# Loading one piece of wo over 121 partitions instead of 128, with other cuts of wo and twelve unread products on PE

## The chip, the core and the metric

The kernel runs on one core of a Trainium2 chip. A core has five engines that run their own instruction lists: PE (TensorE, matrix products), DVE (VectorE), ACT (ScalarE), POOL (GpSimd) and SP (SyncE, which here only issues transfers). Transfers between the chip's memory and the core's SBUF are done by 16 DMA engines. The metric is the device time of one execution in microseconds (us); a smaller number is better.

## The reference

For four sequences and one new token each, the result is a gated mix of two branches of the same input x (4 x 1 x 512):

```
g = sigmoid(sum(x * gate_w))                        # one number for each sequence
a: q = x @ wq                                       # 32 heads of 128
   k, v = the last 4096 rows of the caches          # 8 heads, each shared by 4 heads of q
   a = softmax(q k^T / sqrt(128)) v  @ wo           # wo is 4096 x 512
b: gate = x @ W_gate; up = x @ W_up                 # 512 x 1792
   b = (gate * (gate > 0) * up) @ W_down            # 1792 x 512
out = g * a + (1 - g) * b
```

All inputs and the output are bfloat16. Some 81 MB are read once (the used part of the caches is 64 MB of it), and little is computed with each byte.

## The kernel before, in words

The kernel's instruction lists are written out by hand. A small class, Program, collects the operations of each engine in order (`op` and `dma`) with the names of the events that each waits for; `emit` turns the names into waits on semaphores. What stands first in an engine's list runs first.

**Transfers.** SP issues nearly all loads on one queue, in this order: wq; the keys K of set 0 and 1 and so on in turn with the values V, eight sets (a set is one sequence and half of its heads, 4 MB of keys and 4 MB of values); W_gate and W_up; the last values; W_down (`Wd`); and last wo in pieces (line 286). A piece covers all 128 partitions and some of the 32 rows of 512 elements that each partition holds: `WO_CUTS = (0, 18, 26, 30, 32)` makes pieces of 18, 8, 4 and 2 rows. wo lands in the memory of `KT`, which holds the turned keys before; so SP waits until the scores of the last set are done (`("SC", NSET - 1, 1)`) before it issues wo's pieces. Each piece has an event of its own, `("WO", k)`. ACT issues the two small loads of x and gate_w at the start (lines 272 and 273).

**Each of eight sets.** DVE turns the keys (line 376), PE makes the scores (L384), DVE and PE find the maximum, ACT takes the exponential into `p` (L402), PE spreads `p` with the constant `perm` into four banks of PSUM (L405), ACT copies and DVE turns them, and PE multiplies them with V into `OB` (L426). DVE adds up `OB` (L435, L438). PE runs the eight sets as a loop, with what follows behind it.

**The end, on PE, in order.** After the last set: 14 products of branch b with `Wd` into the bank `SB` (`grouped`, L517); `select` (L442), which gathers the attention's result; DVE's `normal` (L448 to L451: reciprocal, scaling, transpose into `oT`); a transpose on PE (L524); DVE's copy into `oq` (L525). Then come the 18 rows of wo's first piece, as `grouped` products of 512 columns, four column groups of the array side by side, added into the same bank `SB` (L517). ACT copies `SB` into `part` (L529). The rest of wo is used in quarters: for each row four products of 128 columns into four corners of the bank `AB` (L536), row by row as the pieces land. After the second piece's rows, four products with the constant `S32` (L542, 32-bit, two instructions each) add `part` to `AB`. After the last row DVE and ACT copy the four corners to `outr` (L547), and SP stores it (L567).

```
for k in range(1, len(WO_CUTS) - 1):              # L533
    for i in range(WO_CUTS[k], WO_CUTS[k + 1]):
        for q in range(4):                        # a product waits for ("WO", k) and ("OQ",)
```

Of the kernel before, what the change touches and what calls it, by code (L numbers as in the profile page):

```python
# [15 lines left out]
NSET = 8  # L16
NFT = FF // 128
# [2 lines left out]
FAR = 1.0e9  # L20
LOWEST = -3.0e38

WO_CUTS = (0, 18, 26, 30, 32)
GROUPED = 18


# [147 lines left out]
def bass_gated_mix__sliding_block_cached__glu_gated_reglu__decode_kernel(  # L174
# [13 lines left out]
    with ExitStack() as ctx:  # L188
        def sb(name, shape, dt):
            return ctx.enter_context(nc.sbuf_tensor(name, shape, dt))  # L190

        def ps(name, width):
            return ctx.enter_context(nc.psum_tensor(name, [128, width], FP32))
# [14 lines left out]
        perm = sb("perm", [128, 4, 128], BF16)  # L208
# [15 lines left out]
        p = sb("p", [128, 512], BF16)  # L224
# [4 lines left out]
        rows = sb("rows", [128, 4], FP32)  # L229
# [3 lines left out]
        oq = sb("oq", [128, 32 * 32], BF16)  # L233
# [4 lines left out]
        OB = ps("OB", 512)  # L238
# [11 lines left out]
        part = Kw[:, 0, 3 * FQ:3 * FQ + 512]  # L250
        Wo = KT[:, :].bitcast(BF16).rearrange("p (i w) -> p i w", w=512)
# [3 lines left out]
        P = Program()  # L255
# [19 lines left out]
        for s in range(1, NSET):  # L275
# [5 lines left out]
        P.dma("sp", lambda e: e.dma_start(Wd[:, :, :].rearrange("p i w -> p (i w)"),  # L281
                                          B_W_down.rearrange("(p i) w -> p (i w)", p=128)), ("WD",))
        wo_src = A_wo.rearrange("(p i) w -> p i w", p=128)
        for k in range(len(WO_CUTS) - 1):
            lo, hi = WO_CUTS[k], WO_CUTS[k + 1]
            P.dma("sp", lambda e, lo=lo, hi=hi: e.dma_start(  # L286
                Wo[:, lo:hi, :].rearrange("p i w -> p (i w)"),
                wo_src[:, lo:hi, :].rearrange("p i w -> p (i w)")), ("WO", k), [("SC", NSET - 1, 1)])

        P.op("pool", lambda e: e.memset(xz[:, :, :].rearrange("p t w -> p (t w)"), 0.0), ("XZ0",))  # L290
        P.op("pool", lambda e: e.memset(onesf[:, :], 1.0), ("ONESF",))
# [47 lines left out]
        for t in range(4):  # L339
            for half in range(2):  # L340
                for g in range(4):
# [3 lines left out]
                        start=(t == 0), stop=(t == 3), tile_position=(0, 32 * g)),  # L345
                        ("Q",) if (half == 1 and t == 3 and g == 3) else None, [("V", -1), ("XT",)])
        P.op("act", lambda e: e.copy(qrow[:, :], PB[:, 0:1024]), ("QR",), [("Q",)], sem="pro")
        for half in range(2):
            for g in range(4):
                P.op("pe", lambda e, half=half, g=g: e.matmul(  # L350
                    PB[:, 512 * g:512 * g + 512], rall[:, 128 * g:128 * g + 128], qrow[:, 512 * half:512 * half + 512],
                    start=True, stop=True), ("R", half) if g == 3 else None,
# [88 lines left out]
        def select(s):  # L441
            P.op("pe", lambda e: e.matmul(FO[0:16, 256:385], S16[:, :], osum[:, :], start=True, stop=True), ("SEL", s),  # L442
                 [("OSB", s), ("S16",)])

        def normal(s):
            b, half = s // 2, s % 2
            r = slice(32 * b, 32 * b + 32)
            P.op("dve", lambda e: e.reciprocal(rc[:, :], FO[0:16, 384:385]), ("RC", s), [("SEL", s)])  # L448
            P.op("dve", lambda e: e.tensor_scalar(on[32 * b:32 * b + 16, :], FO[0:16, 256:384], rc[:, 0:1], gsb[0:16, b:b + 1],
                                                  op0=ALU.mult, op1=ALU.mult), ("ON", s), [("RC", s), ("G",), ("ON0",)])  # L450
            P.op("dve", lambda e: e.transpose(  # L451
                oT[r, 64 * half:64 * half + 128].rearrange("p (j f) -> p f j", f=4),
                on[r, :].rearrange("p (f i) -> p f i", f=4)), ("OT", s), [("ON", s)], sem="vd" if s == NSET - 1 else None)
# [61 lines left out]
        def grouped(n, stat, mov, waits):  # L515
            g = n % 4
            P.op("pe", lambda e: e.matmul(SB[32 * g:32 * g + 32, :], stat, mov, start=(n < 4), stop=(n >= total - 4),  # L517
                                          tile_position=(0, 32 * g)), ("GR",) if n == total - 1 else None, waits)

        for i in range(NFT):  # L520
            grouped(i, hT[:, i:i + 31 * NFT + 1:NFT], Wd[:, i, :], [("WD",), ("H",)])
        select(NSET - 1)
        normal(NSET - 1)
        P.op("pe", lambda e: e.transpose(FO[:, 128:256], oT[:, 0:128], identw[:, :]), ("CB",), [("OT", NSET - 1), ("IDENTW",)])  # L524
        P.op("dve", lambda e: e.tensor_copy(oq[:, 0:128], FO[:, 128:256]), ("OQ",), [("CB",), ("OQ0",)], sem="vd")  # L525
        for i in range(GROUPED):
            k = max(k for k in range(len(WO_CUTS)) if WO_CUTS[k] <= i)
            grouped(NFT + i, oq[:, i:i + 31 * 32 + 1:32], Wo[:, i, :], [("WO", k), ("OQ",)])
        P.op("act", lambda e: e.copy(part[:, :], SB[:, :]), ("PART",), [("GR",)], sem="va")  # L529
        def quarter(q):  # L530
            return AB[32 * q:32 * q + 4, 128 * q:128 * q + 128]

        for k in range(1, len(WO_CUTS) - 1):  # L533
            for i in range(WO_CUTS[k], WO_CUTS[k + 1]):
                for q in range(4):
                    P.op("pe", lambda e, i=i, q=q: e.matmul(  # L536
                        quarter(q), oq[:, i:i + 97:32], Wo[:, i, 128 * q:128 * q + 128],
                        start=(i == GROUPED), stop=(i == 31), tile_position=(0, 32 * q)),
                        ("ACC",) if (i == 31 and q == 3) else None, [("WO", k), ("OQ",)])
            if k == 1:  # L540
                for q in range(4):
                    P.op("pe", lambda e, q=q: e.matmul(quarter(q), S32[:, 0:4], part[:, 128 * q:128 * q + 128],  # L542
                                                       start=False, stop=False, tile_position=(0, 32 * q)), None,
                         [("PART",), ("S32",)])
# [68 lines left out]
```

## Time and profile before

| | us |
|---|---|
| median of three runs (196.69, 196.76, 335.23) | 196.76 |
| the profiled execution | 196.43 |
| its span, from the first to the last instruction | 195.2 |

| engine | busy us | share of the span |
|---|---|---|
| PE | 93.0 | 48% |
| PEld (weight loads, beside PE) | 44.5 | 23% |
| DVE | 116.6 | 60% |
| ACT | 31.6 | 16% |
| POOL | 15.2 | 8% |

The 16 DMA engines moved 81.04 MB at a mean of 415 GB/s. In the page's 40 slices of the span their mean busy share is nine tenths or more in all slices but the first and the last.

How to read the answers: times count from the start of the span, in us. "L517" is line 517 of the kernel before. A row of a timeline has the start, the duration, the engine, the line, the operation, output<-input, shapes and the count; the brackets behind it give the engine's idle time just before and what ended it. PEclk is the share of its full clock that TensorE was granted. The chain of waits follows the work that ended last back to what released it.

### The profile page before, as it was taken

Reading aid. Unit: us, or ns where it says so; the run is one execution under the profiler, and the core shown is the slowest. Engines: PE = TensorE matmul, PEld = TensorE weight load, DVE = VectorE, ACT = ScalarE, POOL = GpSimd, SP = SyncE. Lnnn points to the kernel's source line nnn. Section 1 sums busy time; section 2 is a strip of 40 time slices with the busy share of each in tenths; the row PEclk is TensorE's granted clock in tenths of the full one; section 3 lists DMA queues with packets and bytes.
Section 4 is the critical chain, followed back from the end, with each engine's and each line's share of the span. In section 5 each row is a group of like instructions: output and inputs, shape, how many; then the busy total and the mean of one; then the engine's idle time right before and its main releaser. Section 6 shows DMA issues by size and latency. Waiting matters only on the chain.

```text
span 195.2 us, 2407 instructions
## 1 busy us (share of the span) xinstructions
PE 93.0 (48%) x1005; PEld 44.5 (23%) x1005; DVE 116.6 (60%) x122; ACT 31.6 (16%) x51; POOL 15.2 (8%) x54
## 2 busy tenths in 40 slices
PE   0017525619611961196219611961196229684543
PEld 0012101216101610152016101610151016124212
DVE  0010299699399439943994399449944994264301
ACT  2002360140140014001400140014001400150002
POOL 7007010100100010001000100010001000000000
PEclk9999999666995596579556955596588557955978
DMA  6999999999999999999999999999999999999990
GB/s 215 427 437 450 430 436 450 430 430 436 443 436 430 430 430 436 443 430 430 430 430 430 437 430 430 430 430 430 430 430 430 430 393 432 464 430 403 421 396 24
DMA packets 3494, 81.04 MB, mean 415 GB/s; under 512 B 416, under 2 KB 420, under 8 KB 676
## 3 DMA queue, kind: packets, MB, share of 16 engines
q1 hardware_dynamic: 3464, 81.01, 97.0%
q8 instruction: 1, 0.02, 0.0%
q10 hardware_dynamic: 28, 0.01, 0.0%
q14 instruction: 1, 0.01, 0.0%
HBM read 81.01 MB, written 0.00 MB: 415 GB/s over the span
## 4 chain that ended last, share of the span: by engine, by line
DMA 79%; PE 17%; issue 1%; SPq 1%; ACTq 1%; DVE 0%; DVEq 0%
DMA Vsb<-in_A_v_cache_dram 61%; PE OB L426 13%; DMA KT<-in_A_wo_dram 12%; DMA xs<-in_gate_w_dram 6%; PE SB L384 2%; PE PB L343 2%; SPq L286 1%; ACTq L272 1%; PE FO L330 0%; DVEq L562 0%; DVE xz L323 0%; PE AB L536 0%; DVE zz L325 0%; DVE zr L328 0%; DVE xs L271 0%
## 5 line engine op out<-in xcount | busy, mean ns | idle before, releaser
L376 DVE STREAM_TRANSPOSE KT<-Ksb 128x4096 f32<-128x4096 f32 x16 | 70.9, 4433 | 4.2 <-DMA Ksb<-in_A_k_cache_dram 4.1
L426 PE MATMUL OB<-Vsb,pT 128*32 128x256 bf16 x512 | 27.7, 406 | 54.8 <-DMA Vsb<-in_A_v_cache_dram 54.8
L384 PE MATMUL SB<-KT,qS 128*32 128x512 bf16 x256 | 32.4, 659 | 6.0 <-DVE KT L376 6.0
L426 PEld LDWEIGHTS OB<-Vsb,pT 128*32 128x32 bf16 x512 | 21.3, 142 | 61.3 <-issue 50.2
L402 ACT ACTIVATE p<-SB,negmax 128x512 bf16<-128x512 f32 x8 | 5.5, 687 | 111.7 <-DVE negmax L396 111.7
L417 DVE STREAM_TRANSPOSE pT<-pP 128x1024 bf16<-128x1024 bf16 x16 | 18.7, 1205 | 3.2 <-ACT pP L410 3.2
L410 ACT ACTIVATE pP<-PB 128x1024 bf16<-128x1024 f32 x16 | 16.2, 1019 | 10.8 <-PE PB L405 10.8
L392 DVE TENSOR_REDUCE mx<-SB 128x1 f32<-128x512 f32 x8 | 5.5, 691 | 20.3 <-PE SB L384 20.3
L370 POOL COPY qS<-qT 32x64 bf16<-32x64 bf16 x32 | 7.3, 229 | 123.0 <-PE SB L384 115.6
L384 PEld LDWEIGHTS SB<-KT,qS 128*32 128x32 bf16 x256 | 10.7, 144 | 22.2 <-issue 12.5
L405 PE MATMUL PB<-p,perm 128*128 128x512 bf16 x32 | 10.0, 444 | 8.9 <-ACT p L402 8.9
L435 DVE TENSOR_TENSOR osb<-OB,emask 128x256 f32<-128x256 f32 x8 | 3.4, 423 | 11.6 <-PE OB L426 11.6
L359 DVE STREAM_TRANSPOSE qT<-Wff 128x1024 f32<-128x1024 f32 x2 | 2.4, 1224 | 8.8 <-ACT Wff L354 8.8
L323 DVE STREAM_TRANSPOSE xz<-xs 128x128 bf16<-128x128 bf16 x1 | 0.3, 311 | 12.1 <-DMA xs<-in_gate_w_dram 12.1
L330 PE MATMUL FO<-zr,onesf 128*128 128x4 f32 x2 | 0.6, 363 | 14.1 <-DVE zr L328 14.1
L394 PE MATMUL FO<-identw,mx 128*128 128x128 f32 x16 | 4.2, 348 | 6.4 <-DVE mx L392 6.4
L394 PEld LDWEIGHTS FO<-identw,mx 128*128 128x128 f32 x16 | 2.6, 202 | 14.3 <-DVE mx L392 14.3
L405 PEld LDWEIGHTS PB<-p,perm 128*128 128x128 bf16 x32 | 2.7, 105 | 12.9 <-ACT p L402 10.5
L396 DVE CUSTOM_DVE_ANT_0 mrow<-FO,qmask 128x128 f32<-128x128 f32 x8 | 2.3, 291 | 5.0 <-PE FO L394 5.0
L350 PE MATMUL PB<-Wff,rall 128*128 128x512 bf16 x8 | 3.8, 626 | 3.1 <-ACT Wff L354 2.0
L547 DVE CAST outr<-AB 4x128 bf16<-4x128 f32 x2 | 0.6, 280 | 7.1 <-PE AB L536 7.1
L442 PE MATMUL FO<-osum,S 128*16 128x129 f32 x18 | 4.4, 335 | 0.0
(69 smaller groups left out, 58.4 us busy)
## 6 DMA issues: line engine op xcount, KB each, us to landing
Ksb<-in_A_k_cache_dram SPq DMA_DIRECT2D x8, 4096.0 KB, 24.8
Vsb<-in_A_v_cache_dram SPq DMA_DIRECT2D x8, 4096.0 KB, 15.7
Vsb<-in_A_wq_dram SPq DMA_DIRECT2D x1, 4096.0 KB, 13.3
KT<-in_A_wo_dram SPq DMA_DIRECT2D x1, 2304.0 KB, 20.5
Wff<-in_B_W_gate_dram SPq DMA_DIRECT2D x1, 1792.0 KB, 19.8
Wff<-in_B_W_up_dram SPq DMA_DIRECT2D x1, 1792.0 KB, 23.4
Wd<-in_B_W_down_dram SPq DMA_DIRECT2D x1, 1792.0 KB, 18.2
KT<-in_A_wo_dram SPq DMA_DIRECT2D x1, 1024.0 KB, 22.6
```

Source lines behind the costliest of these rows:

```text
L343: P.op("pe", lambda e, half=half, t=t, g=g, col=col: e.matmul(PB[32 * g:32 * g + 32, 512 * half:512 * half + 512], xT[:, t, :], Vsb[:, col ...
L370: P.op("pool", lambda e, src=src, dst=dst: e.tensor_copy(dst, src[:, :, :, 8 * b, :]), ("QS", s, a), [("QT", half), ("QS", s, a - 1) if a ...
L376: P.op("dve", lambda e: e.transpose(Kn[:, 1024 * u:1024 * u + 1024], Kw[:, s % 2, lo:lo + 4096]), ("KTC", s, u), [("K", s), ("SC", s - 1, ...
L384: P.op("pe", lambda e, u=u, vo=vo, h=h: e.matmul(SB[32 * h:32 * h + 32, :], qS[:, 16 - 16 * u:48 - 16 * u, 4 * h + vo], Kt[:, h // 2, h % ...
L392: P.op("dve", lambda e: e.tensor_reduce(mx[:, :], SB[:, :], AXIS.X, ALU.max), ("MX", s), [("SC", s, 1)], sem="vd")
L394: P.op("pe", lambda e: e.matmul(FO[:, 128:256], mx[:, 0:1].to_broadcast([128, 128]), identw[:, :], start=True, stop=True), ("MT", s), [("M ...
L402: P.op("act", lambda e: e.activation(p[:, :], SB[:, :], ACTF.Exp, bias=negmax[:, par:par + 1], scale=SCALE), ("EXP", s), [("NEGMAX", s)], ...
L405: P.op("pe", lambda e, h=h: e.matmul(PB[:, 512 * h:512 * h + 512], perm[:, h, :], p[:, :], start=True, stop=True), ("PERM", s) if h == 3 e ...
L410: P.op("act", lambda e, k=k: e.activation(pP[:, 1024 * k:1024 * k + 1024].rearrange("p (c r h) -> p c r h", r=8, h=4), PB[:, :].rearrange( ...
L417: P.op("dve", lambda e, k=k: e.transpose(pT[:, :].rearrange("p (u c q) -> p c u q", u=2, c=64)[:, 32 * k:32 * k + 32], pP[:, 1024 * k:1024 ...
L426: P.op("pe", lambda e, g=g, blk=blk, n=n: e.matmul(OB[32 * g:32 * g + 32, 0:256], pT[:, 32 * blk:32 * blk + 32], Vsb[:, 256 * blk:256 * bl ...
L442: P.op("pe", lambda e: e.matmul(FO[0:16, 256:385], S16[:, :], osum[:, :], start=True, stop=True), ("SEL", s), [("OSB", s), ("S16",)])
```

## The change

Three things are different.

1. wo's pieces are 18, 10, 2 and 2 rows instead of 18, 8, 4 and 2.
2. The third piece (2 rows, `FEWER = 2`) is loaded by two transfers: one for the partitions 0 to 120, whose source is written as 11 times 11 lines, and one for the partitions 121 to 127. Both have events of their own, and the products of this piece wait for both. The other pieces are loaded over 128 partitions as before.
3. PE gets 4 products between `select` and the transpose, and 8 more between the transpose and wo's first piece (`IDLE = (4, 8)`). Each multiplies `perm` with `p`, 128x512, into the bank `OB`; nobody reads the result, and they wait for nothing.

```diff
-WO_CUTS = (0, 18, 26, 30, 32)
+WO_CUTS = (0, 18, 28, 30, 32)
+FEWER = 2
+IDLE = (4, 8)
...
+        def load_wo(k, part, first, last, rows):
+            lo, hi = WO_CUTS[k], WO_CUTS[k + 1]
+            src = wo_src[first:last, lo:hi, :]
+            src = src.rearrange("(a b) i w -> a b (i w)", a=rows) if rows else src.rearrange("p i w -> p (i w)")
+            P.dma("sp", lambda e: e.dma_start(Wo[first:last, lo:hi, :].rearrange("p i w -> p (i w)"), src),
+                  ("WO", k, part), [("SC", NSET - 1, 1)])
...
         for k in range(len(WO_CUTS) - 1):
-            lo, hi = WO_CUTS[k], WO_CUTS[k + 1]
-            P.dma("sp", lambda e, lo=lo, hi=hi: e.dma_start(
-                Wo[:, lo:hi, :].rearrange("p i w -> p (i w)"),
-                wo_src[:, lo:hi, :].rearrange("p i w -> p (i w)")), ("WO", k), [("SC", NSET - 1, 1)])
+            if k == FEWER:
+                load_wo(k, 0, 0, 121, 11)
+                load_wo(k, 1, 121, 128, 0)
+            else:
+                load_wo(k, 0, 0, 128, 0)
...
+        def unread(n):
+            for _ in range(n):
+                P.op("pe", lambda e: e.matmul(OB[:, :], perm[:, 0, :], p[:, :], start=True, stop=True))
+
         select(NSET - 1)
+        unread(IDLE[0])
         normal(NSET - 1)
         P.op("pe", lambda e: e.transpose(FO[:, 128:256], oT[:, 0:128], identw[:, :]), ("CB",), [("OT", NSET - 1), ("IDENTW",)])
+        unread(IDLE[1])
...
-            grouped(NFT + i, oq[:, i:i + 31 * 32 + 1:32], Wo[:, i, :], [("WO", k), ("OQ",)])
+            grouped(NFT + i, oq[:, i:i + 31 * 32 + 1:32], Wo[:, i, :], [("WO", k, u) for u in range(2 if k == FEWER else 1)] + [("OQ",)])
...
-                        ("ACC",) if (i == 31 and q == 3) else None, [("WO", k), ("OQ",)])
+                        ("ACC",) if (i == 31 and q == 3) else None, [("WO", k, u) for u in range(2 if k == FEWER else 1)] + [("OQ",)])
```

## The prediction

> **What bounds the kernel now.** I read the chain of waits first, for the engine on which the end hangs.
>
> ```profile
> DMA 79%; PE 17%; issue 1%; SPq 1%; ACTq 1%; DVE 0%; DVEq 0%
> ...
> 168.79 23.55 DMA KT<-in_A_wo_dram
> 192.34 0.04 issue
> 192.39 0.32 PE AB L536 x8
> ```
>
> The load of wo's last piece lands at 192.34, and only eight small products, the copies and the store follow. Next, the timeline of PE and of ACT's one copy from 182.5 on (start, duration, engine, line, count; in brackets the idle time before it and what ended that).
>
> ```profile
> 182.53 1.09 PE L517 MATMUL SB<-Wd,hT 128*32 128x512 bf16 x14 [1.09 <-DMA Wd<-in_B_W_down_dram]
> 183.45 0.38 PE L442 MATMUL FO<-osum,S 128*16 128x129 f32 x2
> 184.95 0.33 PE L524 MATMUL FO<-identw,oT 128*128 128x128 f32 x1 [1.12 <-DVE oT L451]
> 188.02 2.35 PE L517 MATMUL SB<-KT,oq 128*32 128x512 bf16 x18 [2.75 <-DMA KT<-in_A_wo_dram]
> 190.41 0.59 ACT L529 COPY Ksb<-SB 128x512 f32<-128x512 f32 x1 [14.59 <-PE SB L517]
> 190.51 0.85 PE L536 MATMUL AB<-KT,oq 128*4 128x128 bf16 x32
> 191.19 0.39 PE L542 MATMUL AB<-Ksb,S 128*4 128x128 f32 x8
> 191.75 0.40 PE L536 MATMUL AB<-KT,oq 128*4 128x128 bf16 x16 [0.17 <-DMA KT<-in_A_wo_dram]
> 192.39 0.29 PE L536 MATMUL AB<-KT,oq 128*4 128x128 bf16 x8 [0.23 <-DMA KT<-in_A_wo_dram]
> ```
>
> Each group on KT starts when a piece of wo has landed: 188.02, 190.51, 191.75, 192.39. The gaps 2.49, 1.24 and 0.64 belong to 8, 4 and 2 rows, so a row costs 0.31 us. PE waits 0.17 and 0.23 before the last two groups: the transfers, and not PE, set the end. The windows of these microseconds (stretch, then busy time of PE, PEld, DVE, ACT, POOL, PEclk, share of the 16 DMA engines, GB/s) tell how many engines are still at work.
>
> ```profile
> 190.40:190.60 0.20, 0.09 (x8) 0.09 (x12) 0.00 (x0) 0.19 (x1) 0.00 (x0) 0.50 0.50 184
> 190.60:190.80 0.20, 0.20 (x15) 0.20 (x16) 0.00 (x0) 0.20 (x1) 0.00 (x0) 0.50 0.22 82
> 190.80:191.00 0.20, 0.20 (x16) 0.20 (x12) 0.00 (x0) 0.20 (x1) 0.00 (x0) 0.50 0.08 31
> 191.20:191.50 0.30, 0.30 (x20) 0.09 (x8) 0.00 (x0) 0.00 (x0) 0.00 (x0) 1.00 0.07 27
> 191.50:191.80 0.30, 0.13 (x8) 0.05 (x8) 0.00 (x0) 0.00 (x0) 0.00 (x0) 1.00 0.05 20
> 192.00:192.40 0.40, 0.17 (x16) 0.01 (x5) 0.00 (x0) 0.00 (x0) 0.00 (x0) 1.00 0.00 0
> ```
>
> A share of 0.50, then 0.22, 0.08 and 0.07: one sixteenth is 0.06, so from about 190.9 to 191.9 **one engine alone** still moves data. Fifteen are done about 1 us earlier, and every piece of wo is waited for on this laggard.
>
> **The change part by part.** *How many engines carry the piece over 121 partitions?* The packet counts of the queues answer for the shapes that are there.
>
> ```profile
> q1 hardware_dynamic: 3464, 81.01, 97.0%
> ...
> q10 hardware_dynamic: 28, 0.01, 0.0%
> ```
>
> q1 has 24 loads over 128 partitions and the store of 4 lines, 24 x 128 + 4 = 3076 lines; the other 388 packets are 24 x 16 + 4, one ending packet for each engine that takes part. q10 has the gate's two inputs, 16 + 4 lines, and 8 = 4 + 4 endings, although the first fills 16 partitions: its source has 4 as outer count. So the number of engines divides the outer counts of both sides: 16 of 128, 4 of 4 and 16, 4 of 4. For 121 lines with 11 x 11 in the source that gives 11 engines of 11 lines each, and 7 engines of one line for the rest; five engines get nothing of this piece. [...] No row here shows which engines they are.
>
> *The transfers, on the laggard.* Piece 2 has 10 rows instead of 8: it lands at 188.02 + 10 x 0.311 = 191.13, 0.62 later than now. A line of 2 rows costs 0.64 / 8 = 0.08. If the laggard is one of the five spared engines, piece 4 follows piece 2 directly: 191.13 + 0.64 = 191.77, that is 0.62 before today's 192.39. If it is among the eleven, it takes 11 lines (12, if also one of the last seven): 191.13 + 0.88 + 0.64 = 192.65, or 192.73, so 0.26 to 0.34 later than now. The fifteen others now end near 190.9 and get up to 4 lines more, 0.32; with today's 0.4 from the laggard's last byte (about 191.9) to the landing (192.34) they land by about 191.6 and stay behind 191.77.
>
> *PE after piece 2.* PE now has more to do behind a later landing: 40 products, the four 32-bit ones of L542 (eight instructions), 8 products, 8 products. At full clock 16 products take 0.40 and 8 take 0.29, so 8 more cost 0.11, 0.055 a row, and 0.18 is the tail of any group. Then 10 rows are 0.55; L542 0.39 - 0.17 = 0.22; piece 3 0.11; piece 4 0.11 + 0.18. From 191.13 the sum is 191.13 + 0.55 + 0.22 + 0.11 + 0.29 = **192.30**, against 192.39 + 0.29 = 192.68 now: 0.38 us less. Of the 0.62 that the transfer gives, 0.24 is eaten by PE, which becomes what is late next. At half clock the terms double, (0.55 + 0.22 + 0.11 + 0.11) x 2 + 0.2 = 2.18, and the end is 193.31, 0.63 later than now.
>
> *The unread products.* Twelve products of 128x512 over the whole array; the trace has such a shape at L405.
>
> ```profile
> L405 PE MATMUL PB<-p,perm 128*128 128x512 bf16 x32 | 10.0, 444 | 8.9 <-ACT p L402 8.9
> ```
>
> A mean of 444 ns each includes the tail of a pipelined product, and both clocks; 14 grouped products, four abreast, took 1.09 at full clock, 18 took 2.35 at half: about 0.21 and 0.43 per step of 512 columns. The first four then take 0.85 in the 1.12 that PE waits for DVE; the transpose L524 is not late. At half clock they take 1.7 and hold it back by 0.6; DVE's copy of oq and the grouped products queue behind it. The next eight take 1.7 (3.4) in the 2.75 until wo's first piece: cover at full clock, up to 1.3 late at half. ACT's copy, 0.59 after the grouped products, has a cover of 3 us until L542. I take nothing for them, with 0 to 0.6 us as ends. They also write OB, whose last reader ran before L442.
>
> *SP* issues one DMA more, before the last piece's; the four issues now end 1.75 us or less after 167.47, the engines reach those bytes after 188. Nothing waits behind them but the final store. Cost nothing.
>
> **The clock** decides between 192.30 and 193.31. The windows in steps of 3.41 us on the grid in which PEclk changes:
>
> ```profile
> 51.09:54.50 3.41, 1.78 (x8) 0.72 (x8) 2.25 (x4) 0.90 (x2) 0.72 (x4) 1.00 0.94 404
> 54.50:57.92 3.42, 0.07 (x1) 0.00 (x0) 3.42 (x2) 1.90 (x4) 0.00 (x0) 1.00 1.07 460
> 129.60:133.01 3.41, 1.60 (x8) 0.46 (x7) 2.55 (x3) 1.67 (x3) 0.13 (x1) 1.00 1.07 461
> 133.01:136.43 3.42, 0.00 (x0) 0.00 (x0) 3.42 (x3) 1.13 (x4) 0.00 (x0) 0.50 1.05 450
> 184.21:187.63 3.42, 0.33 (x1) 0.14 (x1) 0.94 (x3) 0.00 (x0) 0.00 (x0) 1.00 0.95 401
> 187.63:191.04 3.41, 2.88 (x42) 1.26 (x46) 0.00 (x0) 0.59 (x1) 0.00 (x0) 0.50 0.84 335
> 191.04:194.45 3.41, 1.23 (x52) 0.57 (x41) 0.56 (x2) 0.52 (x2) 0.00 (x0) 1.00 0.03 10
> ```
>
> After a stretch with 1.78 us of PE the clock stays at 1.00; after 1.60 or 0.33 it falls to 0.50; 2.88 brings it back. So it needs about 1.7 us in the stretch before. With the unread products PE is busy from 183.8 to about 187.2, so the grouped 18 run at 1.00 and take about 1.3 (1.09 + one step of 0.21), until 189.35; then PE idles until 191.13. A stretch that began at 187.63, as here, would hold only 1.3 and the last products would run at 0.50. A stretch that began before about 186.9 also holds 0.3 or more of the unread products, passes 1.7, and the end runs at 1.00. Without them every position of the grid falls back. Of the 3.41 us of positions some 0.55 give the full clock throughout, 0.2 a part, 0.2 the half clock. That takes the grid to lie anywhere. [...]
>
> **The rivals.** *A, forecast*: the laggard is spared and the clock holds: 0.38 off the profiled execution's 196.43 (span 195.2), that is 196.05; the median of the runs is 196.76, and the same step from it gives 196.38.
> *B, slower*: laggard spared, but the last products at partly or fully half clock. The place is L536 from piece 2 on, the point is 1.7 us of PE in the stretch before; price up to +0.63: 196.6 to 197.4. For it: the grid of this very trace. Against it: a grid at any other place is as likely.
> *C, the change does not do what it says*: the laggard is among the eleven. PE then waits for piece 4 at 192.65 to 192.73, +0.29 of products: 0.26 to 0.34 slower, 197.0 to 197.1; at half clock 197.4. No row names the laggard's number; five engines of sixteen are spared. [...]
> *D, all 121 lines on one engine*: 121 x 0.08 = 9.7 from about 190.1 (191.13 less the 1 us of lag), its piece 4 at 200.4, end 200.7: +8.0, 204.8, 4% slower. It decides, at 2% or 3.9 us, from some 70 lines on one engine. Against it: the packet counts.
>
> **How the numbers follow.** The laggard's number has one loose mark: the chain has the gate's second input landed at 13.22, and wq, issued from 0.80 on, needs 13.3.
>
> ```profile
> 2.39 10.84 DMA xs<-in_gate_w_dram
> ...
> Vsb<-in_A_wq_dram SPq DMA_DIRECT2D x1, 4096.0 KB, 13.3
> ```
>
> So the four engines that carried the gate's inputs (interleaved with wq) were done about 1 us or more before wq's last one, and the laggard is hardly among them. If the four are of the eleven, it is spared in 5 cases of 12. I take 0.6, a judgement. Clock held: 0.55. So A 0.33, B 0.26, C 0.34 (over two times, 0.19 and 0.15), D 0.04, the rest 0.03. A's time is 196.4, its own range 196.0 to 196.7 with the 0.3 by which runs and profiled execution differ. To hold 8 in 10 the range takes B and C in: 196.0 to 197.6. All but D and the rest lie within 2%, about what a measurement of this kernel can tell from no change: faster by over 2% 0.01, within 0.94, slower 0.05.
>
> **What would show it.** q1 should have 3466 packets (121 + 11 and 7 + 7 in place of 128 + 16). In the timeline the group of 40 should start near 191.1 and run without a wait into the last 8 (A), or take over 1 us at PEclk 0.5 (B), or end in a wait for KT near 192.6 (C). The DMA share should no longer show one engine alone for 1 us. The forecast is wrong if the laggard isn't a fixed engine, or if lines over 11 engines run slower than 0.08 us each.

## The result, and the profile after

The changed kernel takes 198.17 us (median of 5 runs, 198.04 to 198.91) against 196.79 for the kernel before. The ratio of the runs is 1.0075, 95% interval 1.0053 to 1.0096: slower by 0.75%, less than 2% but clear of the measurement's noise, and outside the forecast range of 196.0 to 197.6. The profiled execution took 198.04 (span 196.8) against 196.43 (195.2), 1.61 more.

The timeline of the changed kernel, the main rows of PE that answer to those shown of before (start, duration, engine, line, tiles, shapes, count; idle time before and what ended it). Lines are 10 to 16 higher than before: L527 is the grouped product, L534 the unread one, L552 the product by quarters. Where rows are left out stands "...".

```profile
184.71 1.04 PE L534 MATMUL OB<-p,perm 128*128 128x512 bf16 x4
...
186.07 1.89 PE L534 MATMUL OB<-p,perm 128*128 128x512 bf16 x8
188.27 1.30 PE L527 MATMUL SB<-KT,oq 128*32 128x512 bf16 x18 [0.31 <-DMA KT<-in_A_wo_dram]
192.19 1.24 PE L552 MATMUL AB<-KT,oq 128*4 128x128 bf16 x40 [2.63 <-DMA KT<-in_A_wo_dram]
...
193.65 0.64 PE L552 MATMUL AB<-KT,oq 128*4 128x128 bf16 x16
```

The unread products fit their gaps, and the grouped ones take 1.30 instead of 2.35. But from the first product on piece 1 (188.27) to the first on piece 2 (192.19) pass 3.92 us. Before, 8 rows took 2.49; 10 rows should have taken 3.11. The time of the profiled execution divides in three: piece 1 is 0.25 later (188.27 against 188.02), the gap is 1.43 longer (3.92 against 2.49), and from piece 2's start to the last product it is 2.10 against 2.17, 0.07 less. The sum is 1.61. The first 0.25 lies ahead of every changed load: the products with `Wd` already began 0.24 later, at 182.77 against 182.53.

The windows of the changed kernel show where the gap comes from (stretch, busy time of PE, PEld, DVE, ACT, POOL, PEclk, share of the 16 DMA engines, GB/s):

```profile
188.00:189.00 1.00, 0.73 (x16) 0.53 (x18) 0.00 (x0) 0.00 (x0) 0.00 (x0) 1.00 1.00 412
189.00:190.00 1.00, 0.57 (x10) 0.10 (x2) 0.00 (x0) 0.39 (x1) 0.00 (x0) 1.00 0.94 287
190.00:191.00 1.00, 0.00 (x0) 0.00 (x0) 0.00 (x0) 0.19 (x1) 0.00 (x0) 1.00 0.84 203
...
192.20:193.20 1.00, 1.00 (x40) 1.00 (x44) 0.00 (x0) 0.00 (x0) 0.00 (x0) 0.50 0.06 23
```

Between 189 and 191 the DMA engines are still busy (0.94, 0.84), but they move 287 and 203 GB/s instead of 412. They are slow. This is the time in which the 121 lines move. By the second row 16 x 0.84 us go into 203 KB, which is 0.14 us for 2 KB, where the forecast had 0.08.

The trace also has every packet with its own time, and these say the same. Between 189.5 and 191.5 a line of 2 KB took 0.13 to 0.14 us (medians of each half microsecond), in e1 below, which loads the third piece over 128 partitions, 0.08 to 0.09. The laggard's last four lines of piece 2 (10 KB each) took 0.56 to 0.59 us instead of 0.39, together 0.73 us more: nearly all of what the gap has above ten rows (3.92 - 3.11 = 0.81).

From 192.2 to 193.2 one engine (0.06) still carries 23 KB, eleven lines of 2 KB. Eight can be its lines of piece 4, the other three must belong to the third piece: the laggard was not spared in this execution. Its packets show eleven lines of the third piece, then eight of piece 4, at 0.084 us each, since the other engines were nearly done by then. PE hid that, because PEclk had fallen to 0.50 and its own chain ended later.

```profile
q1 hardware_dynamic: 3466, 81.01, 96.5%
```

The 3466 packets of the page are the forecast 121 + 11 and 7 + 7 in place of 128 + 16: eleven engines, then seven.

### The profile page after: what moved, and what is told of

The parts are those of the page before. It is cut to its first block, busy times and chain, and to the rows that moved or that the text cites. A ratio compares the mean times of both kernels' runs of the same rounds, so it can differ in the third digit from the quotient of the medians.

```text
span 196.8 us, 2433 instructions
## 1 busy us (share of the span) xinstructions
PE 95.9 (49%) x1017; PEld 46.3 (24%) x1017; DVE 116.7 (59%) x122; ACT 31.6 (16%) x51; POOL 15.2 (8%) x54
## 3 DMA queue, kind: packets, MB, share of 16 engines
q1 hardware_dynamic: 3466, 81.01, 96.5%
## 4 chain that ended last, share of the span: by engine, by line
DMA 78%; PE 18%; issue 1%; ACTq 1%; DVE 0%; DVEq 0%; SPq 0%
DMA Vsb<-in_A_v_cache_dram 61%; PE OB L436 13%; DMA KT<-in_A_wo_dram 12%; DMA xs<-in_gate_w_dram 6%; PE SB L394 2%; PE PB L353 2%; PE AB L552 1%; ACTq L274 1%; PE FO L340 0%; PE AB L558 0%; DVEq L578 0%; SPq L290 0%; DVE xz L333 0%; DVE zz L335 0%; DVE zr L338 0%
## 5 line engine op out<-in xcount | busy, mean ns | idle before, releaser
L436 PE MATMUL OB<-Vsb,pT 128*32 128x256 bf16 x512 | 28.5, 414 | 55.2 <-DMA Vsb<-in_A_v_cache_dram 55.2
L420 ACT ACTIVATE pP<-PB 128x1024 bf16<-128x1024 f32 x16 | 16.2, 1019 | 10.2 <-PE PB L415 10.2
L415 PE MATMUL PB<-p,perm 128*128 128x512 bf16 x32 | 9.5, 423 | 8.9 <-ACT p L412 8.9
L364 ACT CAST Wff<-PB 128x2048 bf16<-128x2048 f32 x2 | 3.7, 1865 | 4.0 <-PE PB L360 4.0
```

The lines of the kernel that those rows point to most:

```text
L415: P.op("pe", lambda e, h=h: e.matmul(PB[:, 512 * h:512 * h + 512], perm[:, h, :], p[:, :], start=True, stop=True), ("PERM", s) if h == 3 e ...
L420: P.op("act", lambda e, k=k: e.activation(pP[:, 1024 * k:1024 * k + 1024].rearrange("p (c r h) -> p c r h", r=8, h=4), PB[:, :].rearrange( ...
L436: P.op("pe", lambda e, g=g, blk=blk, n=n: e.matmul(OB[32 * g:32 * g + 32, 0:256], pT[:, 32 * blk:32 * blk + 32], Vsb[:, 256 * blk:256 * bl ...
```

## The experiments

The theories: **T1**, the transfer over 11 engines slows every line that moves beside it, and **P**, it does so because its lines collide on their way into SBUF; **T2**, lines of 10 rows are slow; **T3**, the unread products do harm through the clock; **S**, the reads of the 11 x 11 pattern are slow; **F**, few engines are slow. "Gap" is the time from the first product on piece 1 to the first on piece 2. Each time stands beside the kernel before on the same chip (196.72 to 196.87). In e3, e6, e8, g3 and i1 PE began on piece 1 without a pause behind the unread products, so there the gap is understated, by 0.2 us at most. Where the interval of the ratio holds 1, as in e7, the time by itself shows no cost, and the reading rests on the gap.

| run | what it is | median | ratio to before, 95% | gap |
|---|---|---|---|---|
| e1 | 128 lines, unread products, new cuts | 196.74 | 0.9997 (0.9983 to 1.0011) | 3.08 |
| e2 | 121 + 7 lines, no unread products | 197.98 | 1.0059 (1.0042 to 1.0076) | 3.86 |
| e3 | unread products alone | 196.63 | 1.0002 (0.9986 to 1.0017) | 2.41 (8 rows) |
| e4 | new cuts alone | 197.24 | 1.0022 (1.0003 to 1.0041) | 3.08 |
| e5 | changed, 121 lines read in a row | 197.72 | 1.0053 (1.0024 to 1.0083) | 3.89 |
| e6 | changed, 112 + 16 lines | 197.82 | 1.0037 (1.0014 to 1.0061) | 3.62 |
| e7 | changed, 64 + 64 lines | 197.51 | 1.0023 (0.9997 to 1.0050) | 3.92 |
| e8 | changed, 126 + 2 lines | 198.02 | 1.0049 (1.0023 to 1.0075) | 3.53 |
| g3 | changed, 119 + 9 lines | 198.14 | 1.0056 (1.0025 to 1.0087) | 3.83 |
| h1 | changed, 120 + 8 lines | 197.77 | 1.0046 (1.0030 to 1.0062) | 3.95 |
| h2 | changed, 104 + 24 lines | 198.00 | 1.0053 (1.0037 to 1.0069) | 3.87 |
| i1 | changed, even + odd partitions | 196.95 | 1.0005 (0.9980 to 1.0029) | 3.05 |
| g4 | changed, 4 rows over 121 | 199.27 | 1.0123 (1.0086 to 1.0161) | 4.32 (8 rows) |
| g1 | before, Wd in halves | 203.31 | 1.0332 (1.0294 to 1.0370) | |
| g2 | before, Wd even + odd | 196.87 | 1.0007 (0.9992 to 1.0023) | |
| h3 | before, Wd as 120 + 8 | 204.56 | 1.0382 (1.0351 to 1.0414) | |
| h4 | before, Wd as 121 + 7 | 207.03 | 1.0513 (1.0485 to 1.0541) | |
| i2 | before, Wd as 60 + 60 + 8 | 204.54 | 1.0402 (1.0368 to 1.0437) | |

### The parts of the change, one by one

e1: the third piece goes back to one load.

```diff
-FEWER = 2
+FEWER = None
```

> The changed kernel with its third piece loaded over 128 partitions in one transfer again; cuts 18, 10, 2, 2 and the unread products stay. Theory T1 (the transfer over 11 engines slows every line that moves beside it): piece 2 starts its products 10 x 0.31 = 3.1 us after piece 1's, not 3.9 as in the changed kernel; the end is 0.8 to 1.4 us earlier than the changed kernel's, 196.8 with the last products at full clock, up to 197.5 at half. Rival T2 (lines of 10 rows are slow by themselves): the gap stays 3.9 and the time 198.2.

e2: no unread products.

```diff
-IDLE = (4, 8)
+IDLE = (0, 0)
```

> The changed kernel without the twelve unread products. T1: the gap from piece 1's to piece 2's products stays 3.9 us and the time 198.2, since the last products ran at half clock already with the unread products. Rival T3 (the unread products do the harm: they make the grouped products early, PE idles longer and falls to half clock): the last products run at full clock here, about 1 us less, 197.2.

e3: the kernel before with the unread products (`FEWER = None`, the old cuts).

> The kernel before with the unread products alone. T1: pieces land as before, the end hangs on the last landing, 196.8; at half clock the last eight products and their tail cost 0.1 more. T3: PE's work behind piece 2 runs at half clock, and although it is waiting for transfers, the end moves by 0.5 or more, 197.3.

e4: the kernel before with the new cuts (`FEWER = None`, `IDLE = (0, 0)`).

> The kernel before with cuts 18, 10, 2, 2 alone. Piece 2 lands 0.62 later than in the kernel before. T1 with the clock as I read it: no unread products, so the grouped products run at half clock for 2.35 us; if that stretch of 3.41 us then lifts the clock, the end is as before, 196.8; if PE's work behind piece 2 runs at half clock, 0.6 more, 197.4. T2: 0.8 more on top, 198.

The timeline of e1, from piece 1 on:

```profile
188.04 1.30 PE L527 MATMUL SB<-KT,oq 128*32 128x512 bf16 x18 [0.27 <-DMA KT<-in_A_wo_dram]
191.12 1.24 PE L552 MATMUL AB<-KT,oq 128*4 128x128 bf16 x40 [1.79 <-DMA KT<-in_A_wo_dram]
...
192.58 0.64 PE L552 MATMUL AB<-KT,oq 128*4 128x128 bf16 x16
```

Its windows:

```profile
189.00:190.00 1.00, 0.33 (x6) 0.00 (x0) 0.00 (x0) 0.59 (x1) 0.00 (x0) 1.00 0.95 367
190.00:191.00 1.00, 0.00 (x0) 0.00 (x0) 0.00 (x0) 0.00 (x0) 0.00 (x0) 0.98 0.54 199
```

The gap is 191.12 - 188.04 = 3.08, as ten rows at 0.31 should have. T2 falls, and T1 has its 3.1. From 190 on the share falls with the GB/s, because engines are done, not because they are slow. Without the split the time is that of before; with it, it was 1.4 more. In e2, whose unread products are gone, the split still costs: 197.98 against e4's 197.24. So the split is the cause of the loss in both settings, by 0.7 to 1.4 us.

T3 falls too. e3 moves nothing (1.0002). Beside the new cuts, which alone cost 0.2% (e4, 1.0022), the unread products seem to help: e1's median is 0.50 below e4's, though the intervals of the two ratios just overlap. e1's runs spread from 196.35 to 197.44. In the profiled execution, which took 197.40, the clock fell to 0.50 at 191, just before the last products: 2.10 from piece 2's start to the last end. i1 below ran these products at 1.00. The spread of e1's runs fits a clock that falls in some executions and not in others, as between cases A and B of the prediction, though only the profiled executions show their clock.

### What collides

e5: the 121 lines come from 242 consecutive rows of wo, so the third piece holds the wrong rows; destination and engines are unchanged.

```diff
...
+                src = A_wo[0:242, :].rearrange("(a b i) w -> a b (i w)", a=11, b=11)
```

> The changed kernel, but the 121 lines are read from 242 consecutive rows of wo (one unbroken stretch of 242 KB) instead of from lines 32 KB apart; destination and engines as in the changed kernel. It leaves out the right data of the third piece. Theory P (the lines collide on the SBUF side, because 11 lines a engine fall on other partitions than the 8 that an engine writes in a load over 128): the gap from piece 1's to piece 2's products stays near 3.9 us, time 198.2. Theory S (the reads of the 11 x 11 pattern are slow): gap 3.1 to 3.3, time 196.8 to 197.5.

e6, e7 and e8 only change the split, to 112 + 16, 64 + 64 and 126 + 2 lines:

```diff
-                load_wo(k, 0, 0, 121, 11)
-                load_wo(k, 1, 121, 128, 0)
+                load_wo(k, 0, 0, 112, 0)          # e7: 0, 64, 8    e8: 0, 126, 7
+                load_wo(k, 1, 112, 128, 0)        # e7: 64, 128, 8  e8: 126, 128, 0
```

> The changed kernel with the third piece as 112 + 16 lines: 16 engines take 7 lines and one line each (packets on q1 as in one load over 128 plus 16 endings, 3472), so no engine is spared, but the lines of an engine again fall on other partitions than in a load over 128. P: the lines are slow, gap well over 3.1, 3.4 to 3.9, time 197.3 to 198.2. Theory F (it is slow because few engines move the piece): gap 3.1 as in the kernel with the piece over 128, time 196.7 to 197.4.

> The changed kernel with the third piece as 64 + 64 lines, 8 engines with 8 lines each, twice. F: fewer engines than eleven, so slower lines than in the changed kernel, gap 3.9 or more. [...]

> The changed kernel with the third piece as 126 + 2 lines, the first on 7 engines with 18 lines each, and the laggard spared if it is none of these seven. P: the lines collide, gap near 3.9; seven engines end late: 18 x 0.13 to 0.16 = 2.3 to 2.9 for the piece, end near 198.5. F: slower still than with eleven engines. If neither, gap 3.1 and piece 4 lands 0.6 after piece 2 on a spared laggard, 196.5 to 197.4.

The windows of e5:

```profile
189.00:190.00 1.00, 0.40 (x6) 0.00 (x0) 0.00 (x0) 0.56 (x1) 0.00 (x0) 1.00 1.02 279
190.00:191.00 1.00, 0.00 (x0) 0.00 (x0) 0.00 (x0) 0.03 (x1) 0.00 (x0) 1.00 0.89 205
...
192.20:193.20 1.00, 0.97 (x64) 0.76 (x50) 0.00 (x0) 0.00 (x0) 0.00 (x0) 1.00 0.00 0
```

The engines are as slow as in the changed kernel (279 and 205 GB/s), and the gap is 3.89, so S falls: it is not the pattern of the reads. From 192.2 on nothing moves any more. In this execution, which has the same split over eleven engines, the laggard was spared: behind piece 2 its packets are the eight lines of piece 4 alone (17 GB/s from 191.6 to 192.2 and 0 from there to 193.2, where the changed kernel has 51 and 23). So **the laggard is not one fixed engine**, if the eleven are the same ones in all these programs: it changes with the execution, or with the program.

The packets of e7 and e8 correct two of my expectations. Each load ends with one packet for each engine that takes part: e7's page has 3480 = 3464 - 144 + 2 x (64 + 16), e8's 3464 = 3464 - 144 + (126 + 14) + (2 + 2). So e7 used 16 engines, not 8, and e8 14, not 7: the number follows from the 64 and 126 lines, and the way in which I had folded the source did nothing. e6's 3480 is 112 + 16 lines and twice 16 endings; the 3472 that I expected left one set out. With e6 and e7 on 16 engines and nearly as slow (gaps 3.62 and 3.92), "few engines" (F) isn't needed either. This leaves P, but by exclusion: no trace here shows the place where lines meet.

### The price with large lines

g1 loads W_down, 14 KB a line, in two halves and g2 in even and odd partitions; g3 takes 119 + 9 lines for the third piece, g4 four rows over 121 partitions (the old cuts).

```diff
...
+        for u in range(2):
+            at = slice(64 * u, 64 * u + 64)       # g2: slice(u, 128, 2)
+            P.dma("sp", lambda e, at=at: e.dma_start(Wd[at, :, :].rearrange("p i w -> p (i w)"), Wd_src[at, :]), ("WD", u))
```

> The kernel before with W_down (1.8 MB, 4.2 us of all 16 engines) loaded as partitions 0 to 63 and then 64 to 127, 16 engines each; nothing else. P (lines collide where an engine's lines fall on partitions that others write too): a large, clean price, since 14 KB a line move that way: 1.6 to 2 times the 4.2 us, 2.5 to 4 us more, 199.3 to 200.8. If the loss in the changed kernel came from the mixture of line sizes or from lines of 2 KB, and not from the partitions: 196.7.

> As the one before, but W_down's two loads take the even and the odd partitions, so that each spans all 128. [...] If any split other than one load over 128 collides: 199 or more.

> The changed kernel with the third piece as 119 + 9 lines: 7 engines with 17 lines each, and 9 with one. P: with only seven engines writing beside nine others on piece 4, the collisions last about as long; the seven end late, 17 x 0.08 = 1.4 at the least, 2.2 at 0.13 a line, so piece 4 lands 192.6 to 193.4 on them; time 197 to 198.2. Rival: few writers collide little and the laggard, if it is none of the seven, is spared: gap 3.1, 196.5 to 197.

> The changed kernel with the cuts of the kernel before, so that the piece over 121 partitions has 4 rows instead of 2: the dose doubled. P: the excess over the kernel with the unread products alone (196.6) is about twice the changed kernel's excess over the one with its piece over 128 (1.25 to 1.4): 2.2 to 2.8, 198.8 to 199.4, less what the laggard's lead hides. If the price is one of starting such a transfer and not of its bytes: 197.9.

The same window, 178 to 182, in which mostly lines of W_down move, of g1 and then of g2:

```profile
178.00:182.00 4.00, 1.82 (x36) 1.58 (x40) 0.02 (x2) 0.00 (x0) 0.00 (x0) 0.50 0.98 211
```

```profile
178.00:182.00 4.00, 3.36 (x64) 2.63 (x64) 0.04 (x1) 0.00 (x0) 0.00 (x0) 0.57 1.02 435
```

All 16 engines are busy in both (0.98 and 1.02), and both pages count 3480 packets, as for two loads of 64 lines over 16 engines each. In halves they move 211 GB/s, spread over all partitions 435, which the kernel before has as well (437). g1's 6.6 us were more than I had bounded (4). So W_down in consecutive halves moved at about half the rate, and in even and odd partitions it cost nothing (1.0007). What makes the one slow and not the other is not shown.

g3's gap is 3.83: the load over seven engines (3464 = 3464 - 144 + (119 + 7) + (9 + 9) packets) is slow as well. g4 doubles the dose: 199.27 - 196.63 of e3 = 2.6 us, about twice the 1.4 of the changed kernel over e1, so the price grows with the bytes.

### Can an engine be spared cleanly?

h1 and h2 split the third piece into 120 + 8 and 104 + 24 lines, h3 and h4 split W_down into 120 + 8 and 121 + 7.

```diff
...
+                load_wo(k, 0, 0, 120, 0)          # h2: 104
+                load_wo(k, 1, 120, 128, 0)
...
+            at = (slice(0, 120), slice(120, 128))[u]      # h4: 121
```

> The changed kernel with the third piece as 120 + 8 lines: 15 engines with 8 lines each, then 8 engines with one. Theory Q (an engine's lines are consecutive ones; 8 of them are the same partitions that it has in a load over 128, so nothing collides): gap from piece 1's to piece 2's products 3.1 us, time as with the piece over 128, 196.4 to 197.4. Rival R (any load but one over all 128, or over partitions spread evenly, collides): gap 3.5 to 3.9, 197.5 to 198.2.

> The changed kernel with the third piece as 104 + 24 lines: 13 engines with 8 lines each, then 12 engines with 2 each; three engines spared in the first. Q: the 104 are clean, the 24 (a fifth of the bytes) collide for a short time; gap 3.1 to 3.3, 196.4 to 197.5. R: gap 3.5 to 3.9, 197.5 to 198.2.

> The kernel before with W_down as 120 + 8 lines, 14 KB a line. Q: no collisions, eight engines get one line of 0.54 us more, one engine gets eight less; 196.7 to 197.3. R: the price of collisions for 1.8 MB, 2 us or more: 199.

> The kernel before with W_down as 121 + 7 lines: the split of the changed kernel at seven times its bytes. Without collisions 11 lines instead of 8 on eleven engines, 3 x 0.54 = 1.6 us more on these: 198.3. With lines slowed as in the changed kernel (0.13 for 0.08 us): 11 x 0.54 x 1.6 = 9.5 instead of 4.3, 5 us more: 201 to 202.

Theory Q, that eight consecutive lines for each engine keep a load clean, falls: 120 lines over 15 engines (3471 = 3464 - 144 + (120 + 15) + (8 + 8) packets) cost as much as any other split (h1, gap 3.95). The window of h3, then of h4:

```profile
178.00:182.00 4.00, 1.72 (x36) 1.50 (x40) 0.00 (x0) 0.00 (x0) 0.00 (x0) 0.50 0.98 215
```

```profile
178.00:182.00 4.00, 0.33 (x8) 0.33 (x12) 0.00 (x0) 0.00 (x0) 0.00 (x0) 0.68 0.97 199
```

Again full shares and about half of g2's 435 GB/s (215 and 199), although 120 and 121 of the 128 partitions take part. h4 is the changed kernel's split at seven times its bytes: 10.2 us, seven times the 1.4, where I had bounded 5.

The last two put the even steps to the test: i1 uses them for the third piece (64 + 64), i2 for W_down with 60 + 60 + 8 lines, 15 engines.

```diff
...
+                load_wo(k, 0, 0, 128, 0, 2)       # the new sixth argument is the step: partitions 0, 2, ...
+                load_wo(k, 1, 1, 128, 0, 2)       # partitions 1, 3, ...
...
+            at = (slice(0, 120, 2), slice(1, 120, 2), slice(120, 128))[u]
```

> The changed kernel with the third piece as its even and its odd partitions, 64 + 64 lines, 16 engines with 4 lines each, twice. If the even steps over all partitions keep it clean, as with W_down: gap from piece 1's to piece 2's products 3.1 us, 196.4 to 197.4, as with the piece over 128. Otherwise 3.6 to 3.9 and 197.5 to 198.

> The kernel before with W_down as the even ones of the first 120 partitions, the odd ones of them, and the last 8: 60, 60 and 8 lines, 15 engines with 4 lines each, twice, then 8 engines. If the even steps are what keeps a load clean, whatever the number of engines: 196.7 to 197.5. [...]

The timeline of i1, and the window of i2:

```profile
188.22 1.30 PE L527 MATMUL SB<-KT,oq 128*32 128x512 bf16 x18
191.27 0.74 PE L552 MATMUL AB<-KT,oq 128*4 128x128 bf16 x40 [1.75 <-DMA KT<-in_A_wo_dram]
...
192.54 0.29 PE L552 MATMUL AB<-KT,oq 128*4 128x128 bf16 x8 [0.21 <-DMA KT<-in_A_wo_dram]
```

```profile
178.00:182.00 4.00, 1.58 (x32) 1.41 (x36) 0.28 (x2) 0.00 (x0) 0.00 (x0) 0.50 1.03 230
```

i1 is clean (gap 3.05, 196.95; 3480 packets, so 16 engines in each load): it is not the second transfer that costs, and in its profiled execution the clock held (40 products in 0.74 instead of 1.24). i2 is not clean (230 GB/s, 204.54): with 15 engines (3486 = 3464 - 144 + 2 x (60 + 15) + (8 + 8) packets) the even steps did not help. In these runs a load kept its rate only where it went over 16 engines **and** over partitions spread through all 128: 128 lines, or 64 in steps of two. Every split that spares an engine was slow (121, 126, 120, 119, 104 and 60 lines), and 64 consecutive and 112 partitions on 16 engines were slow too (by their gaps, and the 64 by g1's time); those that I measured with large lines (121, 120, 60, 64 consecutive) ran at about half the rate (199, 215, 230 and 211 GB/s for 435). So neither the number of engines nor the set of partitions decides alone. Which lines of which engine meet, and where, isn't shown by a trace that doesn't number its engines; that stays open. No version that I ran beats the kernel before: e3's 196.63 and e1's 196.74 are the same as it.

## Why the prediction was wrong, point by point

Case A had the last product end at 192.30; in the profiled execution it ended at 194.29, 1.99 later. The rows above divide this: 0.81 is the longer gap before piece 2 (3.92 for 3.11), 1.01 the half clock, which rival B had priced (193.31 for 192.30), 0.25 the later piece 1; the products at half clock took 0.08 less than forecast (2.10 for 2.18). The first of these had no place in the prediction, and the runs show that it costs 0.7 to 1.4 us in the medians.

**Eleven engines, seven for the rest:** right (3466 packets). The fold of the source, on which I had put it, is not needed: in e7 and e8 other folds changed nothing, and the number followed from the lines (16 engines for 64, 14 for 126). Which five engines were left out no run shows.

**"A line of 2 rows costs 0.64 / 8 = 0.08", and piece 2 "lands at 188.02 + 10 x 0.311 = 191.13":** this step failed. The price came from a load over 128 partitions, and I used it for a load over 121; and I let piece 2 land as if nothing of the third piece moved beside it. The engines that are ahead start the third piece while the laggard is still on the second. In that time a line of 2 KB took 0.13 to 0.14 us, the engines moved 287 and 203 GB/s, and the laggard's lines of piece 2 were slowed with them, so piece 2 lands late: a gap of 3.92 for 3.11. On the laggard itself the 0.08 was right, since its own eleven lines came when the others were nearly done (0.084 each); the error lies in what the others' lines did to piece 2, which the sum left at nothing. The prediction named slower lines as what would make it wrong, yet gave them no bounds and no chance.

**The laggard is spared (0.6):** it wasn't in the changed kernel's profiled execution, but it was in e5's. So it seems to be no fixed engine, and a choice made from one profile may miss it in the next. The 0.6 was a judgement above the 5 of 12 in the prediction. The 5 of 12 take the four engines of the gate's inputs to be among the eleven, which no run shows; what the profiled executions showed is a laggard that was not spared in the changed kernel and was in e5. And where it was spared, in e5, with the clock at 1.00, the time was still 197.12: case A could not have been reached with lines as slow as these.

**PE behind piece 2:** right. I had 1.17 at full clock and 2.18 at half. e5, which ran at 1.00, took 1.18, from 191.99 to 193.17 by its rows

```profile
191.99 0.74 PE L553 MATMUL AB<-KT,oq 128*4 128x128 bf16 x40 [2.59 <-DMA KT<-in_A_wo_dram]
...
192.77 0.40 PE L553 MATMUL AB<-KT,oq 128*4 128x128 bf16 x16
```

and the changed kernel 2.10 at 0.50.

**The unread products at nothing:** right (e3: 1.0002), and that they hold the clock for the grouped products (1.30 forecast and measured) as well.

**The clock at the end:** the reading of about 1.7 us, an estimate from the rows with 1.60 and 1.78, holds for a clock at 1.00: in the changed kernel's trace the stretch from 51.17 with 1.57 us of PE is followed by 0.50, the one from 129.68 with 1.76 by 1.00. The changed kernel's clock changed at 184.29 and 191.12. The stretch of 3.41 us before 191.12 held 1.56 us of PE, under the 1.7, and the next ran at 0.50:

```profile
187.70:191.12 3.42, 1.56 (x20) 0.63 (x18) 0.00 (x0) 0.58 (x1) 0.00 (x0) 1.00 0.93 306
191.12:194.53 3.41, 2.10 (x64) 1.66 (x64) 0.19 (x1) 0.19 (x1) 0.00 (x0) 0.50 0.11 33
```

In e5 the stretch from 187.15 to 190.57 held 1.75, and the end ran at 1.00. (The prediction's "before about 186.9" is a slip: 0.3 of the unread products and 1.3 are 1.6, under its own 1.7.) The stretches do lie elsewhere from one execution to another: they end at 191.12 here, at 190.97 in e1, at 190.57 in e5 and at 192.74 in i1. That the grid may lie anywhere was my assumption; these four ends agree with it, and more is not shown. In the changed kernel's profiled execution they lay nearly as in the kernel before (191.04), the place for which the prediction had said half clock. There the late piece 2 did not bring the half clock about: on time it would have started at 188.27 + 3.11 = 191.38, behind 191.12 as well. That a late piece 2 brings the half clock more often, since PE pauses longer, is likely but not shown.

**Rival C** (not spared, 197.0 to 197.4) came nearest in sign and size, but partly by luck: its condition held, while its wait for piece 4 did not show, since PE at half clock came to piece 4 later than its landing (no wait stands before the last 16 products). The half clock was **B**'s, and the late piece 2 belonged to no rival. **D** (one engine) did not happen.

## What to carry to other kernels

A transfer's price per byte belonged to its shape here (211 GB/s for W_down in halves, 435 in even and odd partitions): before loads are split by partitions, look whether the new shape still goes over all 16 engines and all partitions, and take the rate from a row of that shape. Read the DMA share beside the GB/s: in the changed kernel a share near 1 with fewer GB/s (0.94 and 287) went with lines that took longer (0.13 to 0.14 us for 2 KB), in e1 a falling share (0.54 and 199) with engines that were done (0.08 to 0.09). The engine that is late may be another in the next execution, so don't shift work away from one that you have seen late once.

## What the runs showed of the hardware that I had not expected

With all 16 engines, W_down in consecutive halves of the partitions ran at half the rate: 211 GB/s (g1) for 435 (g2). Fifteen engines with 120 lines did no better (215, h3). Lines that moved beside the slow ones were slow too: the laggard's own lines of piece 2, which belong to a load over 128, took 0.56 to 0.59 us instead of 0.39, and piece 2 came 0.8 us late. One engine alone was about 1 us behind the fifteen others at the end (share 0.08 and 0.07 in the rows before the change), and it seems not to be a fixed one; where its lag comes from wasn't tested.
